# Linear attention and a gated mixture of experts on one core: q of batches 4 to 7 turned by VectorE and moved by transfers, in a new order

## The chip, the core and the metric

The kernel runs on one core of one Trainium2 chip. A core has TensorE (matrix products and transposes into PSUM), VectorE, ScalarE and GpSimd (elementwise work), SyncE (here it only issues transfers), and 16 DMA engines that move data between HBM and SBUF. Each engine works through its own row of instructions in order and waits on semaphores for the others. The metric is the device time of one execution in microseconds; a kernel's time is the median of its runs. A profiled execution gives one trace, from which durations and waits are read.

## What is computed

```python
# q, k, v: (8 batches, 8 heads, 576 positions, 64), float32
phi = lambda x: np.where(x > 0, x, np.exp(x) - 1.0) + 1.0
q_p, k_p = phi(q), phi(k)
kv  = np.einsum('bhsd,bhse->bhde', k_p, v)
z   = np.sum(k_p, axis=2)
num = np.einsum('bhsd,bhde->bhse', q_p, kv)
den = np.einsum('bhsd,bhd->bhs', q_p, z)[..., None] + 1e-06
x   = (num / den).transpose(0, 2, 1, 3).reshape(8, 576, 512)
# then, per batch, a mixture of experts: w1 (8, 512, 1024), w2 (8, 1024, 512)
logits     = x @ w_gate                      # 8 experts
local_gate = sigmoid(x @ w_local)
# position 0 takes e = argmax(logits); later ones keep the previous e where
# local_gate >= 0.5, and take their own argmax where it is below
out[b, s] = softmax(logits[b, s])[e] * (np.maximum(x[b, s] @ w1[e], 0) @ w2[e])
```

## The kernel before

A batch has 8 heads, worked on in two groups of four; group `n = 2 * batch + j` runs from 0 to 15. A tile of q, k or v has 128 partitions: the positions of two heads (64 partitions each, 9 positions to a partition), times two such pairs (`g`), 9 positions (`c`) and 64 features.

For each group, q and k are loaded into `qraw` (two buffers) and `kraw` (four), 576 KB each. ScalarE makes the exponential (`E`) and the relu in place (`E2`); VectorE joins them into phi (`P`, lines 264 to 279): for k in `kraw`, for q in `fq`, laid out so that one position `c` of two pairs is a 128x128 block. VectorE copies v beside a column of ones (`VC`, `vone`). TensorE sums k times v over positions (`K`, `kvps`, line 297), and VectorE copies the result out (`KC`, `kv`).

The product of q with `kv` needs q with features on partitions. TensorE transposes the blocks: eight of a group in `Q` (`tq`, line 308), and the ninth position of both groups of a batch in `QL` (`tql`, line 322). ScalarE copies them to `qT` (`QC`, line 314, and `QLC`, line 328). Then TensorE multiplies `qT` with `kv`: `N` for the first 512 positions, in halves of 32 matmul records (`nps`, line 349), and `NL` for the last 64 (`npl`, line 368). VectorE divides (`D`, `DL`, lines 334 to 337) into `xb`. TensorE transposes that once more (`X`, `XL`), VectorE copies it to `xT` (`XC`, `XLC`), and TensorE makes the logits (`R`, `lps`).

From the logits of position 0 VectorE picks the batch's expert (`PK`); GpSimd loads its weights (`W`) into one of three places, unless they are there; VectorE copies them to where TensorE reads them (`CW`). TensorE makes the hidden layer in eight steps (`H`, `hps`, line 532), ScalarE the relu to bf16 (`HC`, `hT`, line 539), TensorE the output in five (`O0`, `O`, `yps`), ScalarE scales it (`OC`), SyncE stores it (`ST`). `S1` to `S3` make the softmax. At the end a flag says whether any position took another expert than its batch's first; if so, a general path runs (not with these inputs).

The order of all of it is written out in the table `ORDER`: each word is a step, a number behind a slash the PSUM place that its result takes (four places of two banks). Each engine, and SyncE's queue of transfers, gets its instructions in the order of this table. `Lk`, `Lv`, `Lq` are the loads. The table of `fills` puts idle matmuls in front of a few first steps.

Of the kernel before, what the change touches and what calls it, by code (L numbers as in the profile page):

```python
# [11 lines left out]
F32 = mybir.dt.float32  # L12
# [16 lines left out]
HC.0.1 H.0.3/0 HOLD P.k.2 HC.0.2 Lq.4 QL.1/1 H.0.4/3 Lq.5 QLC.1 KC.3 VC.2 HC.0.3 Lk.5 Q.3/2 Lk.4 CW.0.0
HC.0.4 Q.2/1 S1.0 H.0.5/0 QC.2 H.0.6/3 S2.0 HC.0.5 QC.3 K.2/1 HC.0.6 N.1.1.1/0 KC.2 Lv.6 N.1.0.1/2 D.1.1.1  # L30
E.q.4 NL.1/3 H.0.7/1 D.1.0.1 O0.0/0 HC.0.7 DL.1 E2.q.4 S3.0 O.0.0 XL.1/2 E.q.5 X.1.1/1 XLC.1 P.q.4 O.0.1/3
OC.0.0 E.k.5 XC.1.1 Lq.6 R.1.0/2 Lv.5 N.1.0.0/0 RC.1.0 OC.0.1 Lv.4 PK.1 N.1.1.0/1 E.k.4 O.0.2/2 D.1.1.0
W.1.0 E2.q.5 D.1.0.0 O.0.3/3 E2.k.5 P.q.5 OC.0.2 X.1.0/1 OC.0.3 O.0.4/0 XC.1.0 Lq.7 E.q.6 Lk.7 CW.1.0
R.1.1/2 QL.2/3 Q.4/1 QLC.2 RC.1.1 E2.k.4 CW.0.1 H.1.0/3 OC.0.4 VC.5 Q.5/2 W.1.1 HC.1.0 VC.4 QC.4 H.1.1/0
P.k.4 Lv.7 E.q.7 Lk.6 H.1.2/3 BK.1 H.1.3/1 HC.1.1 P.k.5 HC.1.2 K.4/0 E2.q.6 S1.1 K.5/3 HC.1.3 KC.4 CW.1.1
S2.1 QC.5 H.1.4/0 Lk.9 P.q.6 H.1.5/1 HC.1.4 KC.5 Lq.8 VC.6 N.2.0.1/2 HC.1.5 ST.0.0 NL.2/0 E.k.6 D.2.0.1
N.2.0.0/3 N.2.1.0/1 Lk.8 E.k.7 DL.2 Lv.8 H.1.6/2 ST.0.4 D.2.1.0 H.1.7/0 HC.1.6 S3.1 E2.k.7 XL.2/1 O0.1/2
D.2.0.0 HC.1.7 O.1.0 XLC.2 O.1.1/0 VC.7 OC.1.0 P.k.7 E2.k.6 R.2.0/3 E2.q.7 N.2.1.1/1 P.k.6 K.7/2 E.q.8
RC.2.0 P.q.7 O.1.2/3 E.k.9 KC.7 Lq.9 D.2.1.1 OC.1.1 X.2.0/2 E.k.8 K.6/0 XC.2.0 PK.2 OC.1.2 QL.3/1 Lk.10
X.2.1/2 QLC.3 Lv.9 Q.7/3 E2.k.8 KC.6 W.2.0 XC.2.1 Lk.11 Q.6/1 QC.7 P.k.8 NL.3/0 QC.6 O.1.3/2 DL.3 W.2.1  # L40
E2.q.8 VC.8 R.2.1/3 BK.2 E.q.9 XL.3/1 O.1.4/0 XLC.3 RC.2.1 CW.2.0 R.3.0/1 K.8/3 OC.1.4 E.k.10 VC.9 H.2.0/0
Lk.12 RC.3.0 KC.8 Lv.10 S1.2 H.2.1/1 HC.2.0 PK.3 OC.1.3 N.3.1.1/3 HC.2.1 P.q.8 N.3.1.0/0 W.3.0 E2.q.9
H.2.2/2 D.3.1.0 E2.k.9 Lq.10 H.2.3/1 D.3.1.1 HC.2.2 H.2.4/0 HC.2.3 P.k.9 H.2.5/2 HC.2.4 N.3.0.1/3 P.q.9
HC.2.5 K.9/1 E.q.10 D.3.0.1 Lq.11 N.3.0.0/0 E2.k.10 H.2.6/2 D.3.0.0 Q.9/3 HC.2.6 CW.2.1 S2.2 QL.4/0 Q.8/2
QLC.4 S3.2 W.3.1 QC.9 H.2.7/0 KC.9 VC.10 X.3.1/1 HC.2.7 P.k.10 O0.2/3 E2.q.10 XC.3.1 QC.8 X.3.0/0 P.q.10
O.2.0 NL.4/1 E.k.11 O.2.1/2 XC.3.0 Lq.12 OC.2.0 DL.4 E2.k.11 R.3.1/0 CW.3.0 XL.4/3 O.2.2/1 E.k.12 RC.3.1
XLC.4 E.q.11 O.2.3/0 OC.2.1 OC.2.2 N.4.1.1/3 OC.2.3 N.4.0.0/2 O.2.4/1 D.4.0.0 K.10/0 OC.2.4 D.4.1.1 E2.q.11
R.4.0/2 N.4.0.1/1 Lk.14 KC.10 Lv.11 H.3.0/3 P.q.11 Lv.12 ST.1.0 H.3.1/0 HC.3.0 D.4.0.1 H.3.2/3 ST.2.4 HC.3.1
RC.4.0 BK.3 H.3.3/1 Lv.13 HC.3.2 P.k.11 ST.1.4 QL.5/2 HC.3.3 H.3.4/0 CW.3.1 QLC.5 H.3.5/3 HC.3.4 Lk.13 S1.3
E.q.12 Q.11/1 VC.11 PK.4 HC.3.5 X.4.1/2 H.3.6/0 QC.11 Lq.13 W.4.0 K.11/3 HC.3.6 E2.q.12 N.4.1.0/1 KC.11  # L50
XC.4.1 N.5.1.1/0 E2.k.12 D.4.1.0 W.4.1 NL.5/3 H.3.7/2 S2.3 E.k.14 D.5.1.1 O0.3/1 HC.3.7 S3.3 X.4.0/0 DL.5
O.3.0 Q.10/2 P.k.12 OC.3.0 XL.5/3 O.3.1/1 XLC.5 E.k.13 XC.4.0 P.q.12 QC.10 R.4.1/3 O.3.2/0 CW.4.0 OC.3.1
Lq.14 Lv.14 E.q.13 O.3.3/2 VC.12 RC.4.1 N.5.0.1/1 OC.3.3 K.12/3 OC.3.2 D.5.0.1 O.3.4/2 KC.12 N.5.0.0/0
OC.3.4 R.5.0/1 E2.q.13 N.5.1.0/3 ST.3.4 RC.5.0 D.5.0.0 X.5.1/2 H.4.0/1 Lk.15 D.5.1.0 ST.2.0 H.4.1/0 HC.4.0
BK.4 E.q.14 Lv.15 H.4.2/3 PK.5 HC.4.1 H.4.3/1 P.q.13 HC.4.2 W.5.0 H.4.4/0 E2.k.13 XC.5.1 H.4.5/3 Lq.15
HC.4.3 S1.4 HC.4.4 QL.6/2 VC.13 Q.12/1 S2.4 HC.4.5 P.k.13 H.4.6/0 QLC.6 CW.4.1 H.4.7/3 HC.4.6 QC.12 X.5.0/2
W.5.1 K.13/0 HC.4.7 E2.k.14 N.6.0.0/1 KC.13 XC.5.0 N.6.0.1/3 E.k.15 NL.6/0 D.6.0.1 O0.4/2 E2.k.15 S3.4 O.4.0
E2.q.14 O.4.1/3 D.6.0.0 E.q.15 DL.6 O.4.2/1 E2.q.15 OC.4.0 P.q.15 Q.13/0 OC.4.1 O.4.3/2 QC.13 VC.15 CW.5.0
N.6.1.1/3 OC.4.3 O.4.4/0 P.q.14 OC.4.2 N.6.1.0/2 OC.4.4 H.5.0/1 D.6.1.1 ST.4.4 H.5.1/0 D.6.1.0 HC.5.0 ST.3.0
H.5.2/3 P.k.15 HC.5.1 ST.4.0 X.6.0/1 HC.5.2 QL.7/2 VC.14 R.5.1/0 H.5.3/3 RC.5.1 BK.5 H.5.4/0 P.k.14 HC.5.3  # L60
# [14 lines left out]
def kernel(  # L75
# [35 lines left out]

# [8 lines left out]
    with ExitStack() as main:  # L120
# [831 lines left out]
```

## Time and profile before

| | us |
|---|---|
| median of 3 runs | 223.32 (222.03 to 223.62) |
| the profiled execution | 224.62 |
| its span, first to last instruction | 222.4 |
| TensorE / VectorE / ScalarE / GpSimd busy in it | 206.8 / 151.6 / 153.2 / 12.3 |
| mean granted clock of TensorE | 0.996 |

Busy times are of one engine, so they don't add up to the span. In a row of the table by line, `x16` is the count, then come the time that the group kept its engine busy, the mean of one instruction in ns, and behind the second bar the idle time just before, with what ended it. Matmuls are pipelined: one's duration is longer than its share of the busy time.

The slices of the page show the stretch in which TensorE has no gaps, and that transfers go on nearly to its end (each digit is the busy share in tenths of one fortieth of the span):

```profile
PE   7688689999799999999999999999999999999990
DVE  0688791899698989996695966957957659334000
DMA  5999999377669586999299554999370024990082
```

### The profile page before, as it was taken

The numbers are of one execution on the slowest core, as the hardware profiler recorded it, in microseconds if no ns is written. First come the engines' busy times: TensorE is split into PE (matmuls) and PEld (weight loads), VectorE is DVE, ScalarE is ACT, GpSimd is POOL, SyncE is SP. The second block draws the span as 40 slices with busy tenths as digits, with TensorE's granted clock in tenths as the row PEclk, the third lists the DMA queues.
The fourth block names the chain that finished last, engine by engine and source line by source line (L and its number), as shares of the span: only waits on it lengthen the run. The fifth ranks groups of instructions, "written<-read, shape, count | busy, mean of one in ns | idle before, by whom it ended". The sixth has DMA issues, their size and how long they took to land.

```text
span 222.4 us, 8532 instructions
## 1 busy us (share of the span) xinstructions
PE 206.8 (93%) x3695; PEld 149.7 (67%) x3711; DVE 151.6 (68%) x428; ACT 153.2 (69%) x226; POOL 12.3 (6%) x41
## 2 busy tenths in 40 slices
PE   7688689999799999999999999999999999999990
PEld 2266568658675778875888668875888577657640
DVE  0688791899698989996695966957957659334000
ACT  3897958799788898889569655899553355326630
POOL 4004000000000010010000000110000001100000
PEclk9999999999999999999999999999999999999998
DMA  5999999377669586999299554999370024990082
GB/s 194 385 347 330 218 208 392 126 247 272 233 178 401 174 316 215 208 227 222 67 266 406 198 212 101 376 221 204 113 309 4 3 93 134 186 183 2 27 322 90
DMA packets 24141, 46.77 MB, mean 210 GB/s; under 512 B 2834, under 2 KB 8978, under 8 KB 23202
## 3 DMA queue, kind: packets, MB, share of 16 engines
q1 hardware_dynamic: 16834, 37.51, 48.0%
q0 software_dynamic: 6832, 8.45, 23.2%
q8 instruction: 31, 0.51, 0.9%
q10 hardware_dynamic: 432, 0.20, 0.4%
q14 instruction: 12, 0.10, 0.1%
HBM read 61.88 MB, written 9.44 MB: 321 GB/s over the span
## 4 chain that ended last, share of the span: by engine, by line
PE 84%; DMA 6%; DVE 3%; issue 2%; ACT 2%; SPq 0%; DVEq 0%; ACTq 0%
PE hps L532 27%; PE yps L551 25%; PE nps L349 8%; PE kvps L297 7%; PE tq L308 6%; PE tx L383 3%; PE yps L555 3%; DMA qraw<-in_q_dram 3%; DMA kraw<-in_k_dram 3%; PE lps L416 1%; DVE kraw L271 1%; PE npl L368 1%; PE lps L410 1%; PE fill L705 1%; PE tql L322 1%
## 5 line engine op out<-in xcount | busy, mean ns | idle before, releaser
L532 PE MATMUL hps<-xT,w1cur 128*128 128x288 bf16 x512 | 66.9, 286 | 0.8 <-issue 0.8
L551 PE MATMUL yps<-w2cur,hT 128*128 128x512 bf16 x241 | 58.4, 379 | 0.8
L532 PEld LDWEIGHTS <-w1cur 128*128 128x128 bf16 x512 | 48.7, 98 | 13.7 <-issue 1.3
L539 ACT ACTIVATE hT<-hps 128x576 bf16<-128x576 f32 x64 | 41.2, 652 | 24.3 <-PE hps L532 24.2
L551 PEld LDWEIGHTS <-hT 128*128 128x128 bf16 x256 | 24.1, 98 | 25.5 <-issue 0.2
L565 ACT ACTIVATE yo<-yps,pr 128x512 f32<-128x512 f32 x32 | 21.3, 686 | 12.9 <-PE yps L551 10.1
L276 DVE SCALAR_TENSOR_TENSOR fq<-fq,qraw 128x576 f32<-128x576 f32 (+1 forms) x32 | 22.5, 740 | 2.8 <-ACT qraw L247 2.8
L297 PE MATMUL kvps<-vone,kraw 64*64 64x65 f32 x1152 | 19.9, 220 | 3.2 <-ACT hT L539 1.2
L337 DVE TENSOR_TENSOR xb<-nps,rec 128x512 bf16<-128x512 f32 x32 | 22.1, 691 | 1.1
L349 PE MATMUL nps<-kv,qT 64*64 64x65 f32 x1024 | 21.1, 222 | 1.1 <-ACT qT L314 0.6
L297 PEld LDWEIGHTS kvps<-vone,kraw 64*64 64x64 f32 x1152 | 18.2, 134 | 5.4 <-ACT hT L539 1.5
L314 ACT COPY qT<-tq 128x512 f32<-128x512 f32 x32 | 18.3, 640 | 4.5 <-PE tq L308 4.5
L349 PEld LDWEIGHTS nps<-kv,qT 64*64 64x64 f32 x1024 | 17.6, 134 | 4.9 <-issue 2.7
L241 ACT ACTIVATE ek<-kraw 128x1152 f32<-128x1152 f32 x16 | 18.5, 1162 | 2.6 <-DMA kraw<-in_k_dram 2.2
L241 ACT ACTIVATE fq<-qraw 128x1152 f32<-128x1152 f32 (+1 forms) x16 | 18.5, 1156 | 2.4 <-DMA qraw<-in_q_dram 2.2
L269 DVE SCALAR_TENSOR_TENSOR kraw<-ek,kraw 128x1152 f32<-128x1152 f32 x14 | 18.8, 1346 | 0.3 <-ACT kraw L247 0.3
L247 ACT ACTIVATE qraw<-qraw 128x1152 f32<-128x1152 f32 (+1 forms) x16 | 18.3, 1150 | 0.1
L308 PE MATMUL tq<-ident,fq 128*128 128x128 f32 x128 | 16.4, 274 | 0.0
L247 ACT ACTIVATE kraw<-kraw 128x1152 f32<-128x1152 f32 x14 | 16.4, 1168 | 0.0
L308 PEld LDWEIGHTS tq<-ident,fq 128*128 128x128 f32 x128 | 14.3, 141 | 0.5
L388 DVE COPY xT<-tx 128x1024 bf16<-128x1024 bf16 x16 | 10.8, 681 | 3.5 <-PE tx L383 3.5
L302 DVE COPY kv<-kvps 128x130 f32<-128x130 f32 x16 | 4.6, 289 | 11.3 <-PE kvps L297 11.2
(93 smaller groups left out, 185.5 us busy)
## 6 DMA issues: line engine op xcount, KB each, us to landing
kraw<-in_k_dram SPq DMA_DIRECT2D x16, 576.0 KB, 5.8
vraw<-in_v_dram SPq DMA_DIRECT2D x16, 576.0 KB, 6.4
qraw<-in_q_dram SPq DMA_DIRECT2D x14, 576.0 KB, 6.2
w1s<-in_moe_w_dram POOLq DMA_DIRECT2D x7, 1024.0 KB, 10.5
w2s<-in_moe_w_dram POOLq DMA_DIRECT2D x7, 1024.0 KB, 10.6
out_dram<-yo SPq DMA_DIRECT2D x14, 512.0 KB, 5.4
qraw<-in_q_dram SPq DMA_DIRECT2D x2, 512.0 KB, 8.1
w1cur<-in_moe_w_dram POOLq DMA_DIRECT2D x2, 512.0 KB, 7.3
```

Of the source, the lines that this page charges most:

```text
L241: nc.scalar.activation(e[:, :, c0:c1, :], raw_, Act.Exp)
L247: nc.scalar.activation(raw_, raw_, Act.Relu)
L269: nc.vector.scalar_tensor_tensor(r, e, 1.0, r, Alu.min, Alu.add)
L276: nc.vector.scalar_tensor_tensor(e[:, g], e[:, g], 1.0, r[:, g], Alu.min, Alu.add)
L297: nc.tensor.matmul(ps[g * PH:(g + 1) * PH, t, :W], lhsT=f[h, g, c, :], rhs=vo[h, g, c, :], start=(c == 0), stop=(c == C - 1))
L308: nc.tensor.transpose(ps[:, r, i * P:(i + 1) * P], ex_[n, "q"][:, 1 + i + (NC - 1) * r, :, :], identity=ident)
L337: nc.vector.tensor_tensor(dst, ps[:, :, :, :Dh].rearrange("p g (i t) e -> p g i t e", t=2), rec.rearrange("p g (i t o) -> p g i t o", t=2, ...
L349: nc.tensor.matmul(ps[o * PH:(o + 1) * PH, g, (il * 2 + t) * W:(il * 2 + t + 1) * W], lhsT=qT[n][g * PH:(g + 1) * PH, t, i * P + o * PH:i ...
L532: nc.tensor.matmul(ps[:, u, :HS], lhsT=w1b[:, kk, m * P:(m + 1) * P], rhs=xT[b][:, kk, u * HS:(u + 1) * HS], start=(kk == 0), stop=(kk == ...
L539: nc.scalar.activation(hT[b][:, m, :].rearrange("p (u s) -> p u s", u=2), open_.pop(("H", b, m))[:, :, :HS], Act.Relu)
L551: nc.tensor.matmul(ps, lhsT=hT[b][:, m, i * P:(i + 1) * P], rhs=w2b[:, m, :], start=(m == 0), stop=(m == FK - 1))
L565: nc.scalar.activation(ym[:, i, :], ps, Act.Copy, scale=pr[:, i:i + 1])
```

## The change

From batch 4 on (`TURN = 4`), the two heads of a pair lie beside each other in `qraw`, not on the two halves of the partitions, so q is loaded in two transfers of 64 partitions. After phi, `T` (three VectorE instructions) transposes 32x32 blocks of `fq` back into `qraw`, which is free by then; `SH` (eight SBUF-to-SBUF transfers of 32 partitions, on SyncE's queue) moves the blocks to the partitions where `qT` has them. `Q`, `QC`, `QL` and `QLC` are gone in these batches. `N` reads `qT` at other places, and `NL` takes the last 64 positions in two halves of 32.

```diff
+    TURN = 4
...
         def load_q(n):
             if n < NJ:
                 load(qraw[n % NQR][:, :, 1:, :].rearrange("p g c d -> p g (c d)"), q, n, 1, C)
+            elif n < TURN * NJ:
+                load(qraw[n % NQR].rearrange("p g c d -> p g (c d)"), q, n)
             elif n < B * NJ:
-                load(qraw[n % NQR].rearrange("p g c d -> p g (c d)"), q, n)
+                for g in range(2):
+                    ap = bass.AP(q.tensor, (n * (H // NJ) + 2 * g) * S * Dh,
+                                 [[C * Dh, PH], [S * Dh, 2], [1, C * Dh]])
+                    nc.sync.dma_start(out=qraw[n % NQR][g * PH:(g + 1) * PH].rearrange("p t c d -> p t (c d)"),
+                                      in_=ap)
...
+        def turned(n):
+            return qraw[n % NQR].rearrange("p g c d -> p (g c d)").rearrange("p (b s) -> p b s", b=4)
+
+        def q_turn(n):
+
+            f, t = ex_[n, "q"], turned(n)
+            for r in range(2):
+                nc.vector.transpose(
+                    t[:, :, :SM // 2].rearrange("p b (i k r) -> p r i b k", i=NC - 1, r=2)[:, r],
+                    f[:, 1 + (NC - 1) * r:NC + (NC - 1) * r].rearrange("p i g (h k) -> p i (g h) k", h=2))
+            nc.vector.transpose(t[:, :, SM // 2:], f[:, 0].rearrange("p g (h k) -> p (g h) k", h=2))
+
+        def q_move(n):
+            qT[n] = qtp.tile([P, 2, S], F32, name="qT")
+            for b in range(8):
+                g, o, h = b // 4, b // 2 % 2, b % 2
+                nc.sync.dma_start(
+                    out=qT[n][g * PH + 32 * h:g * PH + 32 * (h + 1), o].rearrange("k (t s) -> k t s", t=2),
+                    in_=turned(n)[g * PH + 32 * o:g * PH + 32 * (o + 1), h::2])
...
+                        u, at = (t, i * P + o * PH) if a < TURN else (o, t * HS + i * PH)
                         for g in range(2):
                             nc.tensor.matmul(
                                 ps[o * PH:(o + 1) * PH, g, (il * 2 + t) * W:(il * 2 + t + 1) * W],
-                                lhsT=qT[n][g * PH:(g + 1) * PH, t,
-                                           i * P + o * PH:i * P + (o + 1) * PH],
+                                lhsT=qT[n][g * PH:(g + 1) * PH, u, at:at + PH],
                                 rhs=kv[n][g * PH:(g + 1) * PH, t, :], start=True, stop=True)
...
-                    for g in range(2):
-                        nc.tensor.matmul(ps[j * PH:(j + 1) * PH, g, t * W:(t + 1) * W],
-                                         lhsT=qT[n][g * PH:(g + 1) * PH, t, SM:],
-                                         rhs=kv[n][g * PH:(g + 1) * PH, t, :], start=True, stop=True)
+                    for o in range(1 if a < TURN else 2):
+                        k, u, at = (PH, t, SM) if a < TURN else (32, o, t * HS + SM // 2)
+                        for g in range(2):
+                            nc.tensor.matmul(ps[j * PH + o * k:j * PH + (o + 1) * k, g, t * W:(t + 1) * W],
+                                             lhsT=qT[n][g * PH:(g + 1) * PH, u, at:at + k],
+                                             rhs=kv[n][g * PH:(g + 1) * PH, t, :], start=True, stop=True)
```

The table of the order is new from its first line on. Its first line and one of the middle:

```diff
-Lk.1 FILL/0 Lk.0 Lv.0 Lq.0 Lv.1 E.k.1 Lq.1 E0.0 CL.0 E.k.0 CL.1 Lk.3 P0.0 VC.0 P.k.0 QL.0/1 QLC.0 E.q.0
+Lk.1 FILL/0 Lq.0 Lq.1 Lk.0 Lv.1 Lv.0 E.k.1 CL.1 E.q.0 P.k.1 E2.q.0 E0.0 P.q.0.0 E.q.1 P0.0 E.k.0 P.q.0
...
+R.2.1/3 HC.2.0 H.2.1/0 D.3.1.0 H.2.2/2 SH.9 HC.2.1 H.2.3/0 RC.2.1 BK.2 HC.2.2 CW.2.1 N.3.1.1/1 HC.2.3
```

ScalarE at the start of the program, before. `vone_77` is the v of group 0 with its ones, `fq_80` the first positions of both groups of batch 0, `kraw_69` and `kraw_68` are k of groups 1 and 0, `qraw_72` and `qraw_73` q of groups 0 and 1:

```order
L241 ACTIVATE ek<-kraw_69 128x1152
L250 ACTIVATE fq_80<-q_79 128x256
L241 ACTIVATE ek<-kraw_68 128x1152
L286 COPY vone_77<-vraw_74 128x18x64
L328 COPY qT<-tql 128x2x64 x2
L241 ACTIVATE fq<-qraw_72 128x2x8x64
L247 ACTIVATE qraw_72<-qraw_72 128x2x512
L241 ACTIVATE fq<-qraw_73 128x2x8x64
```

The same place after:

```order
L248 ACTIVATE ek<-kraw_69 128x1152
L248 ACTIVATE fq<-qraw_72 128x2x8x64
L254 ACTIVATE qraw_72<-qraw_72 128x2x512
L257 ACTIVATE fq_80<-q_79 128x256
L248 ACTIVATE fq<-qraw_73 128x2x8x64
L248 ACTIVATE ek<-kraw_68 128x1152
L335 COPY qT<-tql 128x2x64 x2
L254 ACTIVATE qraw_73<-qraw_73 128x2x512
L293 COPY vone_77<-vraw_74 128x18x64
```

Both q groups now go ahead of the copy of v.

SyncE's queue where q of groups 10, 11 and 12 is loaded, before (line 138 is a load, line 574 and 579 are stores):

```order
L138 DMA kraw_68<-in_k_dram 128x2x576
L138 DMA vraw_75<-in_v_dram 128x2x576
L138 DMA qraw_72<-in_q_dram 128x2x576
L138 DMA qraw_73<-in_q_dram 128x2x576
L138 DMA qraw_72<-in_q_dram 128x2x576
L138 DMA kraw_70<-in_k_dram 128x2x576
```

The same place after, where lines 354 and 154 are the moves of `SH.8` and `SH.9` and the q loads in two parts:

```order
L354 DMA qT<-qraw_72 32x2x288 x8
L139 DMA vraw_76<-in_v_dram 128x2x576
L139 DMA kraw_68<-in_k_dram 128x2x576
L154 DMA qraw_72<-in_q_dram 64x2x576 x2
L354 DMA qT<-qraw_73 32x2x288 x8
L139 DMA kraw_69<-in_k_dram 128x2x576
L154 DMA qraw_73<-in_q_dram 64x2x576 x2
```

The loads of q 10 and 11 now stand behind the moves out of the same buffers, and k loads behind moves too.

VectorE in batch 6 and 7, around phi of q 14 and 15, before (line 276 is phi of q, 288 the copy of v, 494 the copy of an expert's weights, 334 to 337 a division):

```order
L276 SCALAR_TENSOR_TENSOR fq<-fq,qraw_73 128x9x64 x2
L288 COPY vone_78<-vraw_74 128x18x64
L457 TENSOR_LOAD si
L494 ISA
L494 COPY w1cur<-w1s 128x4096
L276 SCALAR_TENSOR_TENSOR fq<-fq,qraw_72 128x9x64 x2
L334 TENSOR_SCALAR den_3169<-nps 128x8
```

The same place after, where line 283 is phi of q, 417 and 428 are copies to `xT`, and 345 and 348 the transposes:

```order
L283 SCALAR_TENSOR_TENSOR fq<-fq,qraw_72 128x9x64 x2
L428 COPY xT<-txl 128x2x2x64
L417 COPY xT<-tx 128x4x256
L486 TENSOR_LOAD si
L523 ISA
L523 COPY w1cur<-w1s 128x4096
L450 COPY lt_all<-lps 128x9
L345 STREAM_TRANSPOSE qraw_72<-fq 128x4x4x32 x2
L348 STREAM_TRANSPOSE qraw_72<-fq 128x4x32
L309 COPY kv<-kvps 128x130
L283 SCALAR_TENSOR_TENSOR fq<-fq,qraw_73 128x9x64 x2
L345 STREAM_TRANSPOSE qraw_73<-fq 128x4x4x32 x2
```

The transposes stand a few operations behind the phi that they follow, in one row with everything else that VectorE does.

More of the change, by code (lines that the diff above doesn't have):

```diff
@@ L29 @@
[L29 to L48, printed above, removed]
@@ L679 @@
         ENG = {"PE": ET.PE, "ACT": ET.Activation, "DVE": ET.DVE, "POOL": ET.Pool, "SP": ET.SP}
-        after = {"DVE": ("FI",), "POOL": ("FI",), "SP": ("ST", B - 1, 2), "ACT": ("OC", B - 1, 2),
-                 "PE": ("O", B - 1, NC - 1)}
-        for e, d in after.items():
+        for e in ENG:
             op(("FR", e), lambda e=e: load_flag(ENG[e]))
```

84 lines of the change are left out of this document (54 added, 30 removed).

## The prediction

> **What bounds the kernel now.** I read the page first, then the busy time by stage, then the chain of waits, and last the rows of the work that the change touches.
>
> ```profile
> span 222.4 us, 8532 instructions
> PE 206.8 (93%) x3695; PEld 149.7 (67%) x3711; DVE 151.6 (68%) x428; ACT 153.2 (69%) x226; POOL 12.3 (6%) x41
> PE 84%; DMA 6%; DVE 3%; issue 2%; ACT 2%; SPq 0%; DVEq 0%; ACTq 0%
> ```
>
> TensorE is busy for 93% of the span and holds 84% of the chain. Stage by stage (cut where the first `hps` group of a batch starts; columns after the length: busy TensorE, weight loads, VectorE, ScalarE, GpSimd, granted clock, DMA share, GB/s):
>
> ```profile
> 52.70:84.20 31.50, 29.98 (x710) 23.17 (x711) 27.59 (x71) 27.58 (x39) 1.16 (x5) 1.00 0.74 257
> 84.20:110.50 26.30, 26.20 (x558) 19.62 (x557) 21.73 (x59) 21.88 (x32) 1.82 (x3) 1.00 0.84 195
> 110.50:136.10 25.60, 25.45 (x505) 19.29 (x502) 19.03 (x57) 17.96 (x27) 0.27 (x3) 1.00 0.69 241
> 136.10:158.10 22.00, 21.95 (x357) 15.99 (x356) 17.65 (x51) 18.68 (x28) 1.71 (x3) 1.00 0.96 230
> 158.10:183.60 25.50, 25.39 (x489) 19.08 (x488) 16.71 (x55) 10.97 (x21) 0.37 (x4) 1.00 0.28 110
> ```
>
> From 84.2 to 183.6 us TensorE is busy 98.99 of 99.4 us at full clock. The transposes of batches 4 to 7 lie there, so what is taken from TensorE there shortens the run as far as nothing else comes late. VectorE has 75.1 us of work in the same 99.4 us (21.73 + 19.03 + 17.65 + 16.71): it is the next limit.
>
> **The change part by part.** Durations are of the profiled execution, which took 224.62 us, 2.2 more than its span; the median of the runs is 223.32, 1.3 below it. I add up against 224.62 and take the 1.3 off at the end.
>
> *Taken from TensorE.* In the chain of waits, where a piece's time runs to the next piece's start:
>
> ```profile
> 124.98 0.87 PE tq L308 x8
> 142.14 0.22 PE tql L322 x2
> 147.78 0.23 PE npl L368 x16
> 190.60 0.45 PE tx L383 x8
> 191.04 0.98 PE hps L532 x8
> 155.90 0.63 PE nps L349 x32
> 154.18 1.73 PE yps L551 x8
> 119.07 1.21 PE kvps L297 x72
> ```
>
> Eight `tq` groups go (8 x 0.87 = 6.96 us), and four `tql` groups (4 x 0.22 = 0.88). `npl` gets twice the matmuls, at 32 columns each instead of 64, in four batches: 0.92 us more by its row, 0 if the halves run side by side. I take the row. Sum: -6.9 us, all on the path; the end that is still better is -7.8.
>
> *Taken from ScalarE, given to VectorE.*
>
> ```profile
> L314 ACT COPY qT<-tq 128x512 f32<-128x512 f32 x32 | 18.3, 640 | 4.5 <-PE tq L308 4.5
> L328 ACT COPY qT<-tql 128x128 f32<-128x128 f32 x16 | 3.5, 273 | 3.2 <-PE tql L322 3.0
> L337 DVE TENSOR_TENSOR xb<-nps,rec 128x512 bf16<-128x512 f32 x32 | 22.1, 691 | 1.1
> L302 DVE COPY kv<-kvps 128x130 f32<-128x130 f32 x16 | 4.6, 289 | 11.3 <-PE kvps L297 11.2
> L288 DVE COPY vone<-vraw 128x1152 f32<-128x1152 f32 x15 | 11.6, 781 | 0.0
> L269 DVE SCALAR_TENSOR_TENSOR kraw<-ek,kraw 128x1152 f32<-128x1152 f32 x14 | 18.8, 1346 | 0.3 <-ACT kraw L247 0.3
> ```
>
> ScalarE loses 16 x 0.64 + 8 x 0.27 = 12.4 us of copies and was not the limit, so I cost that at nothing. VectorE gains three block transposes for each q group: two with 512 elements per partition and one with 128. No trace shows this operation. From below: the plain copy moves 1152 elements in 0.78 us, so in proportion 1152 elements of transposing cost 0.78. From above: 512 elements as dear as the two-source operation's 1152, 1.35 us, and the small one 0.4, together 3.1. I take 2 x 0.69 + 0.29 = 1.67 us, the rows nearest in size; 13.4 us for eight groups. With that, VectorE has 88.5 us of work in a stretch that shrinks to 92.5 (99.4 - 6.9): 96% full, and it still fits, since it is in-order work whose consumers stand some microseconds later. Cost on the path: 0. The upper end is the rival on the slower side.
>
> [...]
>
> *The transfers.* Each group's eight moves stand on SyncE's queue, 64 more instructions, and the q load that follows into the same buffer must wait until they have landed, since the transposes write into `qraw`. The rows that bound this:
>
> ```profile
> 158.07 1.12 SPq L579 DMA_DIRECT2D out_dram<-yl  x2
> 140.74 0.37 SPq L138 DMA_DIRECT2D qraw<-in_q_dram  x1
> DMA to landing us min/median/max: 1.9/3.2/9.3
> DMA to landing us min/median/max: 3.9/6.3/8.0
> out_dram<-yo SPq DMA_DIRECT2D x2, 256.0 KB, 2.8
> 150.71 1.15 ACT L241 ACTIVATE fq<-qraw 128x1152 f32<-128x1152 f32 x1
> L539 ACT ACTIVATE hT<-hps 128x576 bf16<-128x576 f32 x64 | 41.2, 652 | 24.3 <-PE hps L532 24.2
> ```
>
> The first landing row is of the 64 KB `yl` stores from 100 us on, the second of the 576 KB q loads between 86 and 160 us. Eight issues at 0.37 to 0.56 us: 3.0 to 4.5, middle 3.7. The last part lands after 1.9 to 3.2, middle 2.5. Then the next q half is issued (0.4), and 288 KB land after 2.8 (the 256 KB row) to 6.3, middle 4.5. From the first move to the next q in place: 8.1 to 14.4 us, middle 11.1. Before, the last q was loaded 10 us ahead of its exponential (issued 140.74, used 150.71) with nothing ahead of it.
>
> Two places in the new order are tight. The load of q 11 follows the moves of q 9 (`SH.9`). Behind its exponential, `E.q.11`, ScalarE has `HC.2.7`, and TensorE's `O.2.0` needs that. Between the two TensorE has five `hps` groups, five `nps` halves, two `tx`, a short `lps` (0.2), a doubled `npl` (0.46) and seven `yps` matmuls (1.5): 4.9 + 3.15 + 0.9 + 0.2 + 0.46 + 1.5 = 11.1 us. The other way takes 11.1 + 1.15 + 0.65 = 12.9 (9.9 to 16.2). TensorE waits 1.8 us (0 to 5.1). The second place is `SH.13` to q 15: TensorE has 10.4 us up to `E.q.15` (two `hps`, two `tx`, two `kvps`, four `nps` halves, `npl`, eight `yps`, `lps`) and three more `yps` groups, 5.2, until `XL.6` needs the bank that `OC.4.1` frees; the other way is 11.1 + 0.4 and about 3.3 of ScalarE: 14.8 against 15.6. Nothing in the middle, 2.5 at the upper end. Sum of this term: +1.8, from 0 to 7.6. The matmuls that use q 8 to 15 have other TensorE work between them and the first of their moves: least for q 11, 5.7 us (two `tx`, three `hps`, `kvps` and an `nps` half), then 6.9 for q 15, against 4.9 to 7.7 for issue and landing. I cost these at nothing; at the upper end q 11 would cost 2.0, the place being the one where a late q 11 has been paid for once.
>
> [...]
>
> *The start.* The new order also moves the first microseconds:
>
> ```profile
> 5.25 1.16 ACT L241 ACTIVATE ek<-kraw 128x1152 f32<-128x1152 f32 x1 [2.21 <-DMA kraw<-in_k_dram]
> 7.31 0.42 ACT L250 ACTIVATE fq<-q 128x256 f32<-128x256 f32 x1 [0.90 <-DMA q<-in_q_dram]
> 8.69 1.14 ACT L286 COPY vone<-vraw 128x1152 f32<-128x1152 f32 x1
> 9.95 0.43 ACT L328 COPY qT<-tql 128x128 f32<-128x128 f32 x2
> 10.27 1.07 ACT L241 ACTIVATE fq<-qraw 128x1024 f32<-128x1024 f32 x1
> 11.37 1.06 ACT L247 ACTIVATE qraw<-qraw 128x1024 f32<-128x1024 f32 x1
> 14.37 0.46 PE L368 MATMUL npl<-kv,qT 64*64 64x65 f32 x16
> 17.22 0.30 PE L410 MATMUL lps<-wg,xT 128*64 128x9 bf16 x8
> 26.36 0.56 PE L416 MATMUL lps<-wg,xT 128*128 128x9 bf16 x16
> 26.89 3.36 PE L532 MATMUL hps<-xT,w1cur 128*128 128x288 bf16 x26
> ```
>
> `vone` of the first group was ScalarE's fourth operation and done at 9.8; now two k and two q exponentials, two q relus, `fq_80` and the `qT` copies stand ahead: 2 x 1.16 + 2 x 1.07 + 2 x 1.06 + 0.42 + 0.43 = 7.4 us from 5.25, so it is done at 13.8 at best. Then `kvps` (1.21) and `kv` (0.29): `npl` at 15.3 or later instead of 14.37. A division of `nps` (about 1.05: 0.69 and two small operations) now stands ahead of what leads to `lps`, where a 0.68 us phi stood. That is 1.3 to 1.4 us later for the expert of batch 0 and for its weights. I take +1.4. It is 0 if the weights were not what came last: `hps` followed `lps` at 26.89 without a gap. It is 2.7 if the first six loads come later in their new order.
>
> Sum: 224.62 - 6.9 + 1.4 + 1.8 = 220.9; less 1.3: **219.6 us** against 223.32, 1.7% less.
>
> **The rivals.**
>
> *VectorE becomes the limit* (slower). Place: from batch 2's hidden layer on. At 3.1 us a group the transposes are 25 us, and VectorE has 100.1 us of work where TensorE has 92.5: 7.6 us more, 227.2, and some more if its waits for TensorE do not vanish. It decides from 2.2 us a group ((92.5 - 75.1) / 8). For it: VectorE is 88% busy in the stage from 52.7 already (27.59 of 31.50). Against it: the operation of 512 elements on two sources takes 0.69, and the transpose has one.
>
> *The q buffers set the pace.* There are two; a buffer now goes load, exponential, relu, phi, transpose, moves before the next load. At the upper ends of the transfer rows the waits are 7.6 us: 224.62 - 6.9 + 1.4 + 7.6 - 1.3 = 225.4. For it: DMA share 0.96 in the stage from 136.1, and landings up to 8.0 and 9.3 us. Against: that is a pair of maxima.
>
> *The whole gain stays.* The start costs nothing and no q is late: 216.4, or 215.5 with the halves of `npl` side by side.
>
> *Nothing happens on the path*, since the transposes were covered: 223. The 0.4 us of idle TensorE in 99.4 speak against it.
>
> **How the numbers follow.** Forecast 0.48, own range 217 to 222.5. VectorE 0.17 (225.6 to 231). q buffers 0.20 (222.5 to 227). Whole gain 0.10. Covered 0.05. About 1% is what a measurement tells from no change here: 221.1 to 225.6. Faster: 0.38 of the forecast and 0.10 of the whole gain, 0.48. Within: 0.10 of the forecast, 0.12 of the q buffers, 0.05 covered, 0.27. Slower: 0.17 and 0.08, 0.25. The range, 216 to 228, leaves out the lower half of the whole gain and the upper part of the VectorE case, about 0.15.
>
> **What would show it.** `tq` and `tql` at half their counts with TensorE still above 97% busy from batch 3's hidden layer to batch 6's: the first term is right. Transposes at 0.6 to 0.8 us: VectorE stays below the limit; above 1.0 us I am wrong on the slow side, and VectorE's row would stand in the chain of waits. ScalarE waiting on `qraw` from the DMA before `E.q.11` and `E.q.15`, TensorE on `hT` behind it, is the transfer term; more than 4 us of it would be the second rival. The first `hps` at 28.3 instead of 26.9 shows the start.

## The result and the profile after

The changed kernel takes **262.13 us** (median of four runs, 258.25 to 338.41) against 223.19 of the kernel before on the same chip: a ratio of **1.166**, 95% interval 1.150 to 1.183. The prediction was 219.6, with a range up to 228. The ratio rests on the runs of 262.01 and 258.25 us, whose middle is 260.1, and leaves out that of 338.41, which had a mean granted clock of 0.56, and that of 262.26, more than 1.5% above the fastest. Differences below are taken from 260.1. The profiled execution is the one that took 262.26 us, and its span is 260.6.

The page after, its span, busy times, the granted clock by fortieths of the span, and the chain of waits by engine and by line:

```profile
span 260.6 us, 8688 instructions
PE 216.4 (83%) x3703; PEld 149.8 (57%) x3703; DVE 164.2 (63%) x452; ACT 144.2 (55%) x202; POOL 12.1 (5%) x41
PEclk9979799999999999567999979995999968999998
PE 38%; DMA 26%; SPq 15%; ACT 9%; DVE 5%; issue 4%; ACTq 0%; DVEq 0%
```

TensorE held 84% of the chain before and holds 38% now. Transfers and SyncE's queue, together 6% before, hold 41%. The stages, cut again at the first `hps` of a batch, from that of batch 1 to that of batch 5 (columns as in the prediction):

```profile
60.10:90.70 30.60, 28.31 (x661) 21.07 (x655) 27.28 (x68) 25.61 (x35) 0.27 (x3) 1.00 0.88 267
90.70:129.60 38.90, 28.97 (x501) 19.89 (x501) 22.73 (x65) 17.90 (x24) 1.82 (x3) 0.82 0.70 156
129.60:159.10 29.50, 24.50 (x406) 16.56 (x402) 20.86 (x64) 13.61 (x18) 0.26 (x3) 0.94 0.74 233
159.10:195.30 36.20, 26.77 (x540) 20.14 (x538) 23.01 (x62) 15.72 (x22) 2.01 (x3) 0.91 0.66 143
```

Up to 90.7 us TensorE is about as dense as it was. From there on it is idle 9.9, 5.0 and 9.4 us in a stage, and the granted clock is 0.82, 0.94 and 0.91. How the idle time comes about stands in the chain of waits of the first bad stage (start, length, what):

```profile
94.14 7.71 DMA qraw<-in_q_dram
101.86 6.58 DMA qT<-qraw
...
108.53 7.96 DMA qraw<-in_q_dram
...
116.58 0.10 ACT fq L248
```

and in SyncE's own queue (start, time from the first to the last issue of the piece, count behind the x):

```profile
84.55 7.06 SPq L354 DMA_DIRECT2D qT<-qraw  x8
91.65 0.59 SPq L139 DMA_DIRECT2D vraw<-in_v_dram  x1
92.36 0.42 SPq L139 DMA_DIRECT2D kraw<-in_k_dram  x1
93.30 1.48 SPq L154 DMA_DIRECT2D qraw<-in_q_dram  x2
94.89 7.56 SPq L354 DMA_DIRECT2D qT<-qraw  x8
102.49 0.59 SPq L139 DMA_DIRECT2D kraw<-in_k_dram  x1
103.19 5.97 SPq L154 DMA_DIRECT2D qraw<-in_q_dram  x2
```

Eight moves hold the queue for 7.06 and 7.56 us. The last of the second set is issued at 101.86 and lands 6.58 us later; the second half of the q load behind it (begun at 103.19, ended 5.97 later) can only be issued then, and takes 7.96 to land. So from the first move of group 9 (94.89) to q 11 in place (116.5) it is 21.6 us. ScalarE sits before `E.q.11` for 10.2 us, and TensorE waits for `hT` behind it. The prediction named this place and this row of waits and gave it 11.1 us, 14.4 at most.

TensorE's own waits in that stage are three, 9.9 us together (behind the count, the idle time before and what ended it):

```profile
103.70 0.53 PE L377 MATMUL nps<-kv,qT 64*64 64x65 f32 x6 [3.51 <-ACT hT L568]
108.58 1.10 PE L377 MATMUL nps<-kv,qT 64*64 64x65 f32 x26 [4.35 <-DMA qT<-qraw]
118.33 1.15 PE L377 MATMUL nps<-kv,qT 64*64 64x65 f32 x32 [2.07 <-ACT hT L568]
```

The first is for an `hT` behind `E.q.10`, whose q load stood behind the moves of `SH.8`. In the second, `N` waits for the moves of group 9 themselves. Only the third is the wait behind `E.q.11`, and it is short, since TensorE had already stood still for the other two.

What ScalarE and TensorE waited for of this kind in the whole run, in the table of waits (us in all, times, longest):

```profile
ACT fq L248 <- DMA qraw<-in_q_dram: 30.6, 7, 10.4
...
PE nps L377 <- DMA qT<-qraw: 10.7, 3, 4.3
```

### The profile page after: what moved, and what is told of

It reads as the page before. It is cut to its first block, busy times and chain, and to the rows that moved or that the text cites. A ratio compares the mean times of both kernels' runs of the same rounds, so it can differ in the third digit from the quotient of the medians.

```text
span 260.6 us, 8688 instructions
## 1 busy us (share of the span) xinstructions
PE 216.4 (83%) x3703; PEld 149.8 (57%) x3703; DVE 164.2 (63%) x452; ACT 144.2 (55%) x202; POOL 12.1 (5%) x41
## 4 chain that ended last, share of the span: by engine, by line
PE 38%; DMA 26%; SPq 15%; ACT 9%; DVE 5%; issue 4%; ACTq 0%; DVEq 0%
DMA qraw<-in_q_dram 14%; PE yps L580 13%; PE hps L561 13%; SPq L354 12%; DMA qT<-qraw 5%; DMA out_dram<-yo 5%; PE nps L377 3%; PE kvps L304 2%; DMA kraw<-in_k_dram 2%; PE yps L584 2%; ACT fq L248 2%; DVE xb L364 2%; ACT ek L248 2%; SPq L154 2%; ACT hT L568 2%
## 5 line engine op out<-in xcount | busy, mean ns | idle before, releaser
L561 PE MATMUL hps<-xT,w1cur 128*128 128x288 bf16 x512 | 69.8, 293 | 0.4 <-issue 0.4
L580 PE MATMUL yps<-w2cur,hT 128*128 128x512 bf16 x256 | 64.6, 406 | 5.6 <-ACT yo L594 3.9
L580 PEld LDWEIGHTS <-hT 128*128 128x128 bf16 x256 | 25.8, 104 | 36.0 <-issue 13.4
L377 PE MATMUL nps<-kv,qT 64*64 64x65 f32 x1024 | 23.9, 232 | 22.2 <-DMA qT<-qraw 10.7
L248 ACT ACTIVATE fq<-qraw 128x1152 f32<-128x1152 f32 (+1 forms) x16 | 18.5, 1153 | 30.6 <-DMA qraw<-in_q_dram 30.6
L377 PEld LDWEIGHTS nps<-kv,qT 64*64 64x64 f32 x1024 | 20.6, 144 | 25.6 <-issue 13.1
L304 PE MATMUL kvps<-vone,kraw 64*64 64x65 f32 x1152 | 22.7, 232 | 2.5 <-DVE xT L428 1.4
L304 PEld LDWEIGHTS kvps<-vone,kraw 64*64 64x64 f32 x1152 | 20.7, 146 | 5.4 <-DVE xT L428 1.6
L361 DVE TENSOR_SCALAR den<-nps 128x8 f32<-128x8 f32 x32 | 5.1, 158 | 13.8 <-PE nps L377 13.6
L295 DVE COPY vone<-vraw 128x1152 f32<-128x1152 f32 x15 | 11.5, 767 | 0.4 <-DMA vraw<-in_v_dram 0.4
L345 DVE STREAM_TRANSPOSE qraw<-fq 128x512 f32<-128x512 f32 x16 | 10.4, 689 | 0.7 <-DVE lt_all L450 0.5
```

Of the source, the lines that this page charges most:

```text
L248: nc.scalar.activation(e[:, :, c0:c1, :], raw_, Act.Exp)
L304: nc.tensor.matmul(ps[g * PH:(g + 1) * PH, t, :W], lhsT=f[h, g, c, :], rhs=vo[h, g, c, :], start=(c == 0), stop=(c == C - 1))
L377: nc.tensor.matmul(ps[o * PH:(o + 1) * PH, g, (il * 2 + t) * W:(il * 2 + t + 1) * W], lhsT=qT[n][g * PH:(g + 1) * PH, u, at:at + PH], rhs= ...
L561: nc.tensor.matmul(ps[:, u, :HS], lhsT=w1b[:, kk, m * P:(m + 1) * P], rhs=xT[b][:, kk, u * HS:(u + 1) * HS], start=(kk == 0), stop=(kk == ...
L580: nc.tensor.matmul(ps, lhsT=hT[b][:, m, i * P:(i + 1) * P], rhs=w2b[:, m, :], start=(m == 0), stop=(m == FK - 1))
```

## The experiments

Each ratio is against the kernel before on the same chip, with its 95% interval. Where a diff says nothing else, it is against the changed kernel.

### The moves: one, four or eight issues

**One transfer in place of eight**, same bytes, in the layout in which they lie (the rearranging is left out).

```diff
-            for b in range(8):
-                nc.sync.dma_start(out=qT[n][...32 partitions...], in_=turned(n)[...32 partitions...])
+            nc.sync.dma_start(out=qT[n], in_=qraw[n % NQR].rearrange(...)...)      # all 128 partitions
```

> Each group's eight moves are replaced by one transfer of the whole tile in the layout in which it lies (128 partitions, 576 KB), so the rearranging between partitions is left out and q of batches 4 to 7 is not what N should get; bytes, transposes, waits and order stay. Theory A (SyncE's eight issues of 0.6 us and more a group, with loads queued behind them, set the pace): SH takes one issue of 0.6, loads go out 5 to 6 us earlier in every group, the time falls from 262 to 225 to 235. Theory B (a q load must wait until the moves have landed, with two buffers, whatever they cost to issue): most of the loss stays, 245 or more. Theory C (the new order loses the time by itself): no change, about 260.

Measured: 225.82 us, ratio 1.011 (1.008 to 1.013). 34.3 of the 36.9 us are gone. Its issues and landings, by the tile `qT` on SyncE:

```profile
L352 SPq DMA_DIRECT2D qT<-qraw x8: 487/510/558, 84.0 to 170.2; - x8
...
DMA to landing us min/median/max: 4.1/5.7/6.4
```

The changed kernel's row for the same tile:

```profile
L354 SPq DMA_DIRECT2D qT<-qraw x64: 586/596/1569, 84.5 to 206.6; - x64
...
DMA to landing us min/median/max: 2.0/2.7/7.2
```

A move of 72 KB lands sooner than a whole tile (2.7 against 5.7 us), but its issue takes SyncE just as long (0.60 against 0.51 us), and there are eight.

**One whole transfer and seven small ones**, 32 partitions by 16 elements, to a tile that nobody reads; and the same with **three** small ones.

```diff
+            for b in range(1, 8):        # the other run: for b in (1, 3, 6)
+                nc.sync.dma_start(out=aside[...32 partitions...], in_=turned(n)[..., :8])
```

> Theory A (the count of issues: eight instructions of 0.6 us in a row on SyncE's queue, with the loads and stores behind them): one whole transfer and seven small ones of 32 partitions x 16 elements take 8 issues again, 7 x 0.6 = 4.2 us a group more than the one transfer, 34 us in all on a queue that TensorE's stages wait for: 245 to 262 us. Theory B (the landing of the pieces, for which the next loads of q wait): the bytes still go in one whole transfer of 5.7 us, and the small ones carry 2 KB each: 226 to 232 us, as with the one transfer (225.8). Between 232 and 245 both take part. Left out, as with the one transfer: the rearranging, so the output isn't the reference's.

> One whole transfer and three small ones of 32 partitions x 16 elements (four issues a group; the rearranging is left out). With one issue it was 225.8 us, with eight 263.4: 37.6 us for 56 issues, 0.67 us an issue. Theory A (issues add up one by one): 24 issues more, 225.8 + 24 x 0.67 = 242 us, 238 to 246. Rival (a threshold: the stages have slack for a few issues and break behind that): 226 to 234, or, if the first small ones already break them, over 252.

Measured: 263.37 us with eight issues, ratio 1.175 (1.165 to 1.185), and 234.42 with four (230.33 to 238.05, too scattered for an interval). Seven transfers of 2 KB cost as much as seven eighths of the tile (ratio 1.175 against 1.166): it is the number of issues. Four issues came out below the 238 to 246 that an even price an issue would give, just above the 226 to 234 of the rival with a threshold. By the medians the first three cost 8.6 us and the next four 29; with that scatter the first figure may be anything from 5 to 12.

**The moves on other queues**: all eight on GpSimd's, and four there and four on SyncE's.

```diff
-                nc.sync.dma_start(
+                nc.gpsimd.dma_start(            # the other run: (nc.gpsimd if g else nc.sync)
```

> The eight moves are issued by GpSimd instead of SyncE, the rest is unchanged. Theory A: k and v loads and stores no longer stand behind moves, the next group's moves no longer behind its loads; 225 to 240 unless GpSimd's issue is as slow (its weight loads then wait behind the moves). Theory B: q loads still wait for the landing; 245 or more. Theory C: about 260.

> The changed kernel with four of a group's eight moves on GpSimd's queue and four on SyncE's; all work is done. Four issues on SyncE's queue gave 234.4 with small extra transfers, eight on GpSimd's 245.2. If the length of a group's issues on one queue decides (4 x 0.6 us side by side in place of 8 x 0.6): 232 to 240. If what counts is that both queues stand still for the same landing: 245 or more.

Measured: 245.21 us, ratio 1.101 (1.094 to 1.107), and 242.34, ratio 1.086 (1.079 to 1.092). About 15 to 18 us come back. The first lies at the lower edge of the forecast of 245 or more, the second between its two forecasts. With all moves on GpSimd, SyncE's longest wait is a new one:

```profile
SPq L154 <- DMA qT<-qraw: 54.8, 16, 22.5
```

SyncE is free of the moves, and then stands at the q load until they have landed, with the loads behind it. Splitting them did not reach the 232 to 240 that the issue time alone would give. What the other 19 to 22 us above the kernel before are made of is not shown by these two runs.

### The queue alone, in the order of before

Small transfers beside the kernel before, 64 in all, behind `P.q` of groups 8 to 15, into a tile that nobody reads: first out of `fq`, then out of a constant tile, so that they wait for no engine, then the same on GpSimd's queue.

```diff
+        def beside(n):
...
+            for b in range(8):
...
+                nc.sync.dma_start(out=aside[32 * o:32 * (o + 1), t], in_=f[32 * i:32 * (i + 1), :16])
...
+                if name[:2] == ("P", "q") and len(name) == 3 and name[2] >= 8:
+                    beside(name[2])
...
+                nc.sync.dma_start(out=aside[...], in_=ident[32 * i:32 * (i + 1), :16])     # the second run
...
+                nc.gpsimd.dma_start(out=aside[...], in_=ident[32 * i:32 * (i + 1), :16])   # the third run
```

> Before, and behind P.q of groups 8 to 15 eight small transfers of 32 partitions x 16 elements on SyncE from fq to a tile that nobody reads: 64 issues of 0.6 us, 38 us, on SyncE's queue of before's order, in no cycle with the q buffers (the loads of q wait for nothing new but their place in the queue). If an issue costs wherever the queue has it: 245 to 262. If it costs in the cycle from load to turn to move to load: 222 to 230.

> Before with the 64 small transfers beside (241.7 us), but out of a constant tile: they wait for no engine, their place, count and size stay. If the time goes into the issues themselves, 64 x 0.6 us on SyncE's queue: 238 to 244. If it goes into SyncE standing still until fq is ready (23 us of waits in that profile), with the loads behind it: 222 to 228.

> Before with the same 64 small transfers out of a constant tile, now on GpSimd's queue, which before has 41 instructions and 5% of busy time, in place of SyncE's (240.2 us there). If the cost is the place on SyncE's queue, where the loads of k, v and q and the stores stand behind them: 223 to 227. If it is the transfers themselves on the DMA engines, which all loads share: 235 to 242.

Measured: 241.66 us (ratio 1.079, 1.070 to 1.088), 240.19 (1.071, 1.063 to 1.079), 223.30 (0.996, 0.992 to 1.000). The first lies between its two forecasts (245 to 262, 222 to 230). Between the first two there is no difference clear of noise, so the wait for `fq` costs little; the place on SyncE's queue is worth 17 us. SyncE's queue in the second of the three runs:

```profile
84.49 6.06 SPq L289 DMA_DIRECT2D aside<-ident  x8
90.66 0.52 SPq L139 DMA_DIRECT2D qraw<-in_q_dram  x1
91.22 7.59 SPq L289 DMA_DIRECT2D aside<-ident  x8
98.93 0.55 SPq L139 DMA_DIRECT2D qraw<-in_q_dram  x1
99.52 7.40 SPq L289 DMA_DIRECT2D aside<-ident  x8
108.28 0.37 SPq L139 DMA_DIRECT2D qraw<-in_q_dram  x1
```

and the same place in the kernel before:

```profile
87.83 13.76 SPq L138 DMA_DIRECT2D qraw<-in_q_dram  x3
109.77 0.37 SPq L138 DMA_DIRECT2D kraw<-in_k_dram  x1
```

Three q loads that stood back to back, issued between 87.8 and 101.6 us, are pulled out to 108.3. Transfers that nobody reads and that wait for no engine's result hold the queue ahead of each for 6.06, 7.59 and 7.40 us, and the last load goes out about 7 us later than before. On GpSimd's queue the same 64 leave the time unchanged (ratio 0.996), so in that run the DMA engines had room for them. One issue is small beside its transfer (0.59 us against 5.1 from issue to landing, medians of the second run), but 64 of them in one row cost the kernel 17 us.

### The q buffers

Three q buffers, with two `xT` buffers in place of three for room; the two `xT` buffers alone; and the third q buffer together with the moves on GpSimd.

```diff
-        NQR = 2
+        NQR = 3
...
-    NX = 3
+    NX = 2
```

> Three q buffers (and two xT buffers for room, which the next run has alone). Theory B: the load of q n no longer waits for the landing of the moves of n-2, so 10 us or more come off against the run with two xT buffers alone. Theory A: the issues stay, 64 of 0.6 us, and the load still stands behind them on the queue: within 5 us of that run.

> The changed kernel with two xT buffers in place of three, to read the run before by. Both theories: 262 us or more; by how much more is what the buffer itself is worth here, 0 to 10 us.

> The eight moves on GpSimd's queue and three q buffers (two xT buffers). Each alone gave 245.2 (moves on GpSimd) and 3.8 us off (third buffer). Theory A+B (the loads stand behind the moves on the queue, and behind their landing through the buffers; one hides the other): 226 to 234 us. If the effects only add: about 241. If GpSimd's own issues and the moves' landing are the rest: 240 to 245.

Measured: 255.48 us (ratio 1.141, 1.133 to 1.150), 259.30 (1.154, 1.146 to 1.163), 239.88 (1.070, 1.062 to 1.079). Freeing the q load from the landing of the moves gives some 3 to 4 us by the medians, though the intervals of the two runs overlap; with the moves on GpSimd, the third buffer and the two `xT` buffers together give 5.3. So the two effects roughly add, and one doesn't hide the other. With the moves on SyncE the landing is the small one. With the moves on GpSimd 16 us above the kernel before remain, and SyncE still stands for 48.0 us in all before q loads until moves have landed; what these 16 us are made of stays open.

### VectorE's transposes

Before, with the three transposes behind `P.q` of groups 8 to 15 and nobody who reads them: into the q buffer, and into a tile of their own (two `xT` buffers).

```diff
+            for r in range(2):
+                nc.vector.transpose(t[:, :, :SM // 2]..., f[:, 1 + (NC - 1) * r:NC + (NC - 1) * r]...)
+            nc.vector.transpose(t[:, :, SM // 2:], f[:, 0]...)
```

> Before, and behind P.q of groups 8 to 15 the same three transposes on VectorE into the q buffer, which nobody reads (TensorE's transposes stay; the load of q n+2 waits for them). The cost of 8 x 1.65 = 13.2 us more VectorE by itself. Prediction's step (VectorE's 13 us lie beside other work): within 2 us of before, 222 to 226. The first rival (VectorE becomes the limit): 227 to 237.

> Before with the transposes beside again (234.8 us), but into a tile of their own that nobody reads, so the load of q n+2 no longer waits for them (two xT buffers in place of three, for room; that changed the new kernel by -2.8). If VectorE's time is the cost: 232 to 237. If the longer hold on the q buffer is: 222 to 227. Between: both.

Measured: 234.79 us, ratio 1.051 (1.043 to 1.060), and 230.77, ratio 1.033 (1.027 to 1.040). 13.2 us of new VectorE work cost about 7 us in the order of before, and the longer hold on the q buffer some 4 more (the buffers of `xT` differ between the two runs, and what that is worth in this order was not measured).

The new order without the transposes, once with one transfer straight from `fq` and once with the eight moves (turning left out in both):

```diff
         def q_turn(n):
-            f, t = ex_[n, "q"], turned(n)
-            ...
+            pass
```

> The one transfer a group in the new order (225.8 us), now straight from fq and without the 24 transposes on VectorE: turning and rearranging are left out, so the output isn't the reference's. If VectorE's 13.2 us are what is left between 225.8 and the forecast of 219.6 (VectorE on the path, as in the run of before with the transposes beside, +11 us): 213 to 220. If they lie beside other work in the new order, as the prediction had it: 223 to 226.

> The changed kernel with its eight moves a group straight from fq, without the 24 transposes on VectorE (turning left out, so the output isn't the reference's). With one transfer the transposes were worth 2.6 us (225.8 to 223.2). If VectorE's time and the moves only add: 258 to 261. If the transposes and the wait of the q buffer for the moves behind them lengthen the cycle of the two q buffers: 245 to 255, since here the next load of q waits for fq alone.

Measured: 223.21 us, ratio 0.998 (0.993 to 1.002), and 245.97, ratio 1.099 (1.089 to 1.109). With the runs above, as medians of the runs that the ratios rest on, in us:

| new order | one transfer | eight moves |
|---|---|---|
| without transposes | 223.1 | 245.0 |
| with transposes | 225.8 | 260.1 |

Seven more issues a group cost 21.9 us by themselves. The transposes cost 2.7 beside one transfer and 15.1 beside eight. A likely reason is that with eight moves they stand in a long row between one q load and the next: there ScalarE waits 30.6 us for q loads with transposes, and without them (the waits of ScalarE in that last run):

```profile
ACT fq L248 <- DMA qraw<-in_q_dram: 11.1, 6, 4.6
ACT fq L248 <- issue: 9.4, 1, 9.4
```

11.1, and 9.4 more in one wait for which the profile names no cause. VectorE's time and the shorter hold on the buffer both changed here, and the runs don't part them for eight moves.

### The order

The new order with `Q`, `QC`, `QL` and `QLC` put back, at places that I chose where a PSUM place was free; the order of before with `T` and `SH` right behind each `P.q`, with eight moves and with one transfer.

```diff
-    TURN = 4
+    TURN = 8
...
-Q.7/2 E.k.8 W.2.1 KC.9 T.8 O.1.2/3 E2.k.8 D.3.0.1 SH.8 QC.7 O.1.3/1 P.k.8 E2.q.9 CW.2.0 OC.1.2 O.1.4/0
+W.2.0 NL.3/3 K.9/1 OC.1.1 E.q.9 DL.3 N.3.0.1/0 VC.8 Q.7/2 E.k.8 W.2.1 KC.9 O.1.2/3 E2.k.8 D.3.0.1 QC.7 O.1.3/1
```

> The new order without the turn: Q, QC, QL and QLC of batches 4 to 7 are back on TensorE and ScalarE, put into the new table behind the phi of both groups where a PSUM place is free; no transposes on VectorE, no moves, q loaded in one transfer. Theories A and B (the moves and what waits for them): within 5% of before, 221 to 234, the q load waiting for phi only. Theory C: the loss stays, 245 or more. The start of the new order is in it too: first hps later by 0 to 2.7 us.

> The order of before with the turn: in batches 4 to 7 Q, QC, QL and QLC are taken out, and T and SH stand right behind each group's phi of q. Theories A and B: slower than before by 15 us or more, since the next q load stands right behind the moves here too (240 to 265). Theory C: near before, 216 to 228.

> Order of before, each T and SH right behind P.q, and one transfer a group in place of eight (rearranging left out, so the output isn't the reference's). Theory C (the new order loses what TensorE gains, since the one transfer in the new order gave 225.8 with 200.5 us of TensorE): the 6.9 us of TensorE come off, 215 to 219 us. Rival (the gain doesn't come in any order, as transfers and VectorE take it): 222 to 227. If the order of before is worse for the turn than the new one: over 227.

Measured: 242.58 us (ratio 1.080, 1.075 to 1.086), 259.98 (1.166, 1.160 to 1.173), 248.17 (1.110, 1.102 to 1.119). With eight moves the two orders are alike (a ratio of 1.166 each); with one transfer the new order is 22 us better than the old one, and only 1% above the kernel before. So the new order is not what loses the time. The gain expected of the old one with one transfer did not come: in the chain of waits of that run one `qT` transfer stands for 8.54 us and the q load behind it for 7.64 (from 157.5 to 174.4 us), and SyncE waits 31.9 us in all before q loads until moves have landed. The first of the three lies between its two forecasts (221 to 234, 245 or more); it rests on my places for the four steps and shows only that the new order does not suit the old way of transposing.

## Why the prediction was wrong

**The step that failed is the transfers' term, "+1.8, from 0 to 7.6", with the waits of `N`, which it put at nothing.** The eight issues were sized at 3.7 us, from 0.37 and 0.56 us of other transfers on this queue; they took up to 7.56 us, since a move's issue is 0.60 and the longest take 1.5 (the later sets on SyncE's queue, two of them back to back twice):

```profile
127.78 12.30 SPq L354 DMA_DIRECT2D qT<-qraw  x16
160.74 5.90 SPq L354 DMA_DIRECT2D qT<-qraw  x8
167.43 5.65 SPq L354 DMA_DIRECT2D qT<-qraw  x8
196.87 10.37 SPq L354 DMA_DIRECT2D qT<-qraw  x16
```

The last part was to land after 2.5 us and took 6.6 at the critical place, and the half load after it 8.0 in place of 4.5. That makes 21.6 us where 11.1 was forecast.

Yet the wait that this was to cause, TensorE on `hT` behind `E.q.11`, is 2.1 us, near the 1.8 of the forecast: by luck, since TensorE had already stood still for 7.9 us that the prediction had not counted. In the three stages from 90.7 to 195.3 us TensorE is idle for 24.4 us, by its own waits:

| TensorE idle, 90.7 to 195.3 us | us | in the prediction |
|---|---|---|
| `N` and `NL` until the moves of their q had landed | 11.7 | nothing, 2.0 at the upper end |
| behind a late exponential: `E.q.10` 3.5, `E.q.11` 2.1 | 5.6 | 1.8 for `E.q.11`, `E.q.10` not counted |
| behind the scaling of an output, where ScalarE stood 2.0 us until a store had landed | 4.0 | not counted |
| other | 3.1 | nothing |

The larger mistake is one of kind: I counted the delay at two places where a q load follows its own moves. But loads and stores go out on SyncE's queue in the order of the table, and those behind a set of moves come later as well: k, v and q loads wait for the 7.06 and 7.56 us of `SH.8` and `SH.9` to pass. The runs of before with small transfers show that part with no q dependence at all: 17 us for 64 issues on SyncE, nothing on GpSimd. The prediction asked what each step waits for, and not what stands behind it.

**TensorE's 6.9 us.** The rows are right: `tq` and `tql` have half their counts. The statement that would have shown the gain, TensorE above 97% busy from batch 3's hidden layer to batch 6's, fails: 83% and 74% in the stages from 129.6 and 159.1. Without transposes and with one transfer the new order should have given about 218 (223.32 - 6.9 + 1.4) and gave 223.2. The stages of that run, from batch 2's first `hps` to batch 5's:

```profile
91.00:115.50 24.50, 23.95 (x500) 17.25 (x499) 19.66 (x59) 17.75 (x24) 1.83 (x3) 1.00 1.05 234
115.50:137.10 21.60, 21.60 (x409) 15.40 (x402) 18.96 (x59) 13.55 (x18) 0.27 (x3) 1.00 0.91 315
137.10:162.70 25.60, 24.27 (x541) 17.94 (x540) 20.67 (x59) 15.74 (x23) 1.86 (x2) 1.00 0.89 197
```

They take 71.7 us, and before the three took 73.9: there are 1.9 us of idle TensorE now, and the start is 2.9 us later (first `hps` at 29.8). Over the whole span TensorE's busy time is 203.1 us against 206.8 before, 3.7 less and not 6.9, and its idle time has grown from 15.6 to 17.9. In the run with one transfer and the transposes the busy time is 200.5 us, 6.3 less, and the idle time 23.2. I had taken the gain off as if the new order kept TensorE as dense as the old one; that was not shown by anything. Why the busy time fell by so much less without the transposes stays open.

**VectorE, put at nothing.** The size was right, 1.65 us a group against 1.67:

```profile
L345 DVE STREAM_TRANSPOSE qraw<-fq 128x512 f32<-128x512 f32 x16 | 10.4, 689 | 0.7 <-DVE lt_all L450 0.5
L348 DVE STREAM_TRANSPOSE qraw<-fq 128x128 f32<-128x128 f32 x8 | 2.2, 269 | 0.0
```

That 96% full still fits did not hold: the transposes cost 2.7 us with one transfer, about 7 in the order of before, and 15.1 with the eight moves. The rival in which VectorE becomes the limit was to decide from 2.2 us a group; VectorE cost time at 1.65, and in the changed kernel it is not the limit (63% busy).

**The waits of `N`, put at nothing.** TensorE waited 10.7 us in three `nps` for moves to land, and 1.9 in `npl`; with issue and landing together at 14.1 us (7.56 + 6.58) and not 4.9 to 7.7, the cover of 5.7 to 6.9 us was too short.

**The start** was forecast at +1.4 and measured +2.4 (first `hps` at 29.3 against 26.9); `vone` of group 0 was done at 14.1, forecast 13.8.

**The rivals.** "The q buffers set the pace" has the right place and the right sign in the profile: ScalarE waits 30.6 us for `qraw`, and more than 4 was to mean this rival. Of the 30.6 us, 10.2 stand before `E.q.11` and 10.4 before `E.q.14`; `E.q.15`, the second place of the forecast, has 1.9. But the number of buffers is not what sets the pace: a third one gave 3 to 4 us, and the loads are late by their place on the queue. The rival's price of 225.4 came from the same undersized rows. Against the forecast of 219.6, the 40.5 us up to 260.1 divide by the runs into 3.5 (to 223.1: TensorE's gain and start), 2.7 (transposes) and 34.3 (eight issues in place of one, 12.4 of them only together with the transposes).

**The clock makes it worse.** In the stage from 90.7 the changed kernel's 501 matmul records keep TensorE busy for 28.97 us at a granted clock of 0.82; the run above has 500 in the stage of the same batch in 23.95 at 1.00. So 5.0 of that stage's 14.4 us more are slower matmuls. The three stages together have 1447 records against 1450 and take 32.9 us more: 22.5 are idle time and 10.4 are busy time for the same work, of which an estimated 9.0 follow from the granted clocks of 0.82, 0.94 and 0.91 (23.95, 21.60 and 24.27 us divided by them). The low clock stands in and right behind the long gap (columns as in the stages):

```profile
94.00:103.00 9.00, 6.20 (x114) 4.86 (x112) 6.74 (x26) 3.00 (x4) 1.65 (x2) 1.00 0.94 250
103.00:109.00 6.00, 0.94 (x22) 0.84 (x26) 0.00 (x0) 3.42 (x6) 0.00 (x0) 0.64 1.05 192
109.00:118.00 9.00, 7.26 (x109) 4.40 (x101) 4.97 (x14) 1.43 (x2) 0.00 (x0) 0.67 1.14 253
```

The prediction used full clock throughout.

No version that was run beats the kernel before. Moving the blocks through HBM with fewer issues was not tried.

## What to carry to other kernels

When a change adds transfers, count issues, not bytes: multiply their number by the issue time of the nearest like transfer, and treat the product as busy time of the issuing engine, with everything behind it on that queue late by up to as much (here 0.60 us an issue and up to 7.56 a set of eight, and beside the kernel before a q load about 7 us later). Price the step that reads what is moved as well: here its waits were the largest part of TensorE's idle time. Before taking a queue as free, look at what stands behind the place: here loads with little lead turned its delay into idle time of the engine that bounds the kernel (30.6 us of ScalarE before q, 5.6 of TensorE behind late exponentials), and 64 small transfers cost 17 us on SyncE's queue and nothing on GpSimd's. And a chain that goes round through few buffers (load, exponential, transpose, moves, load) is added up as one sum: the transposes, which cost 2.7 us alone, cost 15.1 where eight moves stood in the same round, though the runs don't show by which way.

## What the runs showed of the hardware

The time of an issue on SyncE's queue did not grow with the size in these runs: by the medians, 0.51 us for 576 KB from SBUF to SBUF, 0.60 for 72 KB, 0.59 for 2 KB; 0.37 for a load of 576 KB from HBM, 0.65 for a half load of 288 KB. The longest move took 1.57. The 64 small transfers on GpSimd's queue, by their tile:

```profile
L289 POOL DMA_DIRECT2D aside<-ident x64: 496/496/1413, 79.2 to 162.5; - x64
...
DMA to landing us min/median/max: 1.7/5.0/10.7
```

Their issue cost GpSimd 0.50 us each, and the kernel nothing (ratio 0.996). And idle time came with a low clock here: in the 6 us that hold TensorE's longest gap the granted clock was 0.64, in the 9 us before them 1.00, in the 9 us behind them 0.67, and over the stage of 39 us that holds the gap 0.82.
